# A weight conversion's mask and product merged into one VectorE operation, and three slots of a hand-written order moved

## The chip, the cores and the metric

The kernel runs on one core of a Trainium2 chip. The metric is device time in microseconds (us) of one execution, the median of three runs. The engines are named as in the profile: PE (TensorE matmul) and PEld (its weight load), DVE (VectorE), ACT (ScalarE), POOL (GpSimd), and SP, which issues DMAs.

## The reference

The computation is a chain of three blocks over 8 batches of 576 tokens, 8 heads of width 64, model width 512:

```python
q_s = softmax of q over its last axis;  k_s = softmax of k over the sequence
kv  = einsum('bhsd,bhse->bhde', k_s, v)
x   = einsum('bhsd,bhde->bhse', q_s, kv)          # linear attention, then (4608, 512)
e_idx = argmax(x @ w_gate)                        # one of 8 experts per token
out[mask] = gate_w * eom * (relu(x[mask] @ w1[e]) @ w2[e])
h   = maximum(maximum(x @ w1, x @ w2), x @ w3)    # second block, 512 -> 768
out = h @ w_out                                   # 768 -> 512
```

q, k, v and the expert weights are float32. The four weights of the last block (`m_w1`, `m_w2`, `m_w3`, `m_wo` in the kernel) are drawn as float64, so the kernel gets each number as two 32-bit words and makes a float32 of them by integer operations. That is the conversion of this document.

## The kernel before, in words

The program has two halves. In the first, up to about 580 us of the trace, attention and the first expert block run interleaved; in the second the last block runs, as a matrix product with saved multiplications (lines 1248 to 1418).

The first half is an order written out by hand in *slots*. Slot 0 to 255 each hold one matmul group of the expert block: 12 matmuls of 288 columns, either `l1_group` (x times w1, line 650, tile `hp`) or `l2_group` (h times w2, line 668, tile `yp`). 32 slots make a batch: 8 of l1, 8 of l2, 8 of l1, 8 of l2. After its group, a slot runs its *events*: the functions that `at(slot, f, ...)` put there, in the order of the calls to `at`. Each engine runs its instructions strictly in the order in which slots and events issue them.

An l1 group ends with two instructions: ACT writes the high part of `h` (line 655), and DVE the low part (line 656). The l2 groups after it need both parts of all four column blocks, so the first l2 group of eight waits, at its tenth to twelfth matmul, for the low part of the seventh l1 group, and the second l2 group for that of the eighth. An l2 group's result leaves PSUM by ACT (line 673) in the first half of a batch and by DVE (line 675) in the second. The pool of these PSUM banks has four.

Attention is cut into *units*: unit n is batch n // 2 and head half n % 2. Unit n starts at slot START[n] = 16n - 51, and STEADY says at which offset from there each of its steps runs, in the order of FRONT and BACK (lines 551 and 552). In what follows "+7" means offset 7 from the unit's start. In every unit from 4 on, the l1 groups are at +3 to +10 and l2 groups at +11 to +18 (the last three are +0 to +2 of the next unit). The steps that matter here:

- q: `q_neg` at -4 (line 233), `q_rows` on ACT, `q_inv` at +6 (lines 244 and 245), `q_norm` at +8 (line 298, DVE, tile `qn`), then at +10 and +15 `q_tr`, the transposes of `qn` on PE (line 350), and `q_lo` (line 365, DVE).
- k and v: `k_max` at -4 (line 224), `k_tr` at +0 (lines 266 to 271; the tile `dg`), `k_exp` at +1 (the PE matmul `kB` of line 278 reads `dg`), `kv_mm` and `kv_norm` at +6 (lines 325 to 337), `kv_lo` at +7 (line 343, DVE).
- `x_mm` at +13 and +17 (line 383, PE), `x_lo` at +14 and +18 (line 401, DVE).
- The expert weights: in every second slot `split_sub` (line 627, ACT) and in the slot after it `split_lo` (line 634, POOL).
- Routing, once a batch, at slots counted from the odd unit: `route_2` at +22, `route_3` at +25, `route_4` at +26 (20 small POOL instructions, lines 491 to 515), and five `route_5` at +27, 29, 31, 33, 35 (line 519, indirect DMAs that POOL issues, all into one table, each after the one before it has landed). In the terms of the next units these are +6, +9, +10 and +11, 13, 15 of an even unit and +1 and +3 of the odd unit behind it.

The conversion has 32 pieces of 128x384 numbers. Each has three steps: `dec_load` (DMA into `draw`), `dec_bits` four slots later (DVE lines 717, 719, 721 make `df` and `dp`; ACT lines 722 and 724 make `da` and `dr`; POOL lines 725 and 726 multiply and add into `dr`), and `dec_store` two slots after that (lines 734 to 736: mask, product, DMA to DRAM). DEC gives the offsets of `dec_bits` in even units (two pieces), odd units (three) and after the last unit (two). The tiles `draw`, `df`, `dp` and `da` have one buffer each, `dr` two. `dec_store` comes last among a slot's events.

Of the kernel before, what the change touches and what calls it, by code (L numbers as in the profile page):

```python
# [14 lines left out]
ALU = mybir.AluOpType  # L15
# [29 lines left out]

STEADY = ((-4, -1, -4, 0, 1, 3, 6, 6, 7, 8), (10, 10, 13, 14, 15), (15, 16, 17, 18, 19))
EARLY = {
    2: ((None, None, None, -8, -5, -3, 0, 0, 3, -1), (2, 3, 3, 7, 5), (5, 6, 7, 8, 9)),  # L50
    3: ((0, 3, 3, 5, 6, 6, 8, 8, 8, 9), (10, 10, 11, 13, 15), (13, 13, 14, 15, 16)),
# [4 lines left out]
ROUTE1 = (17, 19)  # L56

QROWS = (((-2, 4), (-1, 2), (0, 4), (2, 3), (3, 3), (4, 2), (5, 2)), 6)
DEC = ((5, 10), (3, 8, 11), (18, 26))


@with_exitstack
def tile_linear_attention__then__moe(
# [15 lines left out]
    nc = tc.nc  # L79
    dma = nc.sync.dma_start  # L80
    gdma = nc.gpsimd.dma_start
    vec = nc.vector
# [470 lines left out]
    for n, s0 in START.items():  # L553
# [3 lines left out]
        else:  # L557
            t = STEADY
        if n > 2:
# [169 lines left out]
    def dec_store():  # L729
        if not dec_m:  # L730
            return
        i, j, a2, r = dec_m.popleft()

        vec.tensor_scalar(out=a2, in0=a2, scalar1=1.125 * 2.0 ** -15, scalar2=None, op0=ALU.is_ge)
        nc.gpsimd.tensor_tensor(out=r, in0=a2, in1=r, op=ALU.mult)
        dma(out=w32_d[i][:, j], in_=r)

    dslots = [START[n] + o for n in range(4, 2 * B) for o in DEC[n % 2]] + [START[2 * B - 1] + o for o in DEC[2]]
    assert len(dslots) == 32
    for x in dslots:  # L740
        at(x - 4, dec_load)
        at(x, dec_bits)
        at(x + 2, dec_store)
# [782 lines left out]
```

## Time and profile before

| what | value |
|---|---|
| median of three runs | 1200.14 us (1200.04 to 1201.42) |
| the profiled execution's own time | 1197.52 us |
| its span, first to last instruction | 1195.5 us |
| PE busy, share of the span | 1136.8 us, 95% |
| DVE busy | 786.4 us, 66% |
| ACT busy | 583.8 us, 49% |
| POOL busy | 412.9 us, 35% |
| 32 masks on DVE (line 734), median of one | 506 ns |
| 32 products on POOL (line 735), median of one | 1030 ns |

The shares are means over the whole span. The conversion runs from 86 us to 530 us, and there DVE and POOL are far busier than their means. "Busy" of PE is the union of its matmuls, which overlap each other.

### The profile page before, as it was taken

The numbers are of one execution on the slowest core, as the hardware profiler recorded it, in microseconds if no ns is written. First come the engines' busy times: TensorE is split into PE (matmuls) and PEld (weight loads), VectorE is DVE, ScalarE is ACT, GpSimd is POOL, SyncE is SP. The second block draws the span as 40 slices with busy tenths as digits, with TensorE's granted clock in tenths as the row PEclk, the third lists the DMA queues.
The fourth block names the chain that finished last, engine by engine and source line by source line (L and its number), as shares of the span: only waits on it lengthen the run. The fifth ranks groups of instructions, "written<-read, shape, count | busy, mean of one in ns | idle before, by whom it ended". The sixth has DMA issues, their size and how long they took to land. (4 is left out here: it accounts for less than half of the span.)

```text
span 1195.5 us, 21865 instructions
## 1 busy us (share of the span) xinstructions
PE 1136.8 (95%) x7626; PEld 1061.4 (89%) x7626; DVE 786.4 (66%) x1476; ACT 583.8 (49%) x1549; POOL 412.9 (35%) x502
## 2 busy tenths in 40 slices
PE   4699999999999999999999999999999999999994
PEld 2499899898999999999998899899899989989983
DVE  7777878788787878647798566455556446554430
ACT  2466676756667676536454423443344244333220
POOL 2156857677676857787241020000000000000000
PEclk8799999999999999999999999999999999999997
DMA  6784657576565654437698478487678848747701
GB/s 160 187 226 127 195 156 212 156 221 201 160 193 165 187 143 153 135 137 249 212 320 298 160 236 287 134 295 237 225 231 266 272 147 287 237 138 235 222 19 42
DMA packets 204210, 234.97 MB, mean 197 GB/s; under 512 B 78253, under 2 KB 122061, under 8 KB 204096
## 3 DMA queue, kind: packets, MB, share of 16 engines
q1 hardware_dynamic: 202384, 233.14, 62.7%
q8 instruction: 62, 1.02, 0.4%
q0 software_dynamic: 1712, 0.39, 0.2%
q14 instruction: 52, 0.43, 0.1%
HBM read 189.56 MB, written 44.13 MB: 195 GB/s over the span
## 5 line engine op out<-in xcount | busy, mean ns | idle before, releaser
L668 PE MATMUL yp<-h,w 128*128 128x288 f32 x1536 | 222.7, 299 | 7.4 <-DVE h L656 7.4
L668 PEld LDWEIGHTS yp<-h,w 128*128 128x128 f32 x1536 | 207.7, 188 | 11.4 <-DVE h L656 8.8
L650 PE MATMUL hp<-xs,w 128*128 128x288 f32 x1536 | 217.5, 298 | 0.0
L650 PEld LDWEIGHTS hp<-xs,w 128*128 128x128 f32 x1536 | 206.9, 188 | 2.6
L634 POOL TENSOR_TENSOR w<-stg,w 128x512 fp32r<-128x512 f32 x126 | 180.3, 1436 | 79.6 <-ACT w L627 78.1
L1248 PE MATMUL pY<-t,sw 128*128 128x384 f32 (+1 forms) x972 | 193.5, 342 | 2.1 <-ACT s L1257 1.7
L1248 PEld LDWEIGHTS pY<-t,sw 128*128 128x128 f32 x972 | 172.8, 188 | 6.3 <-ACT s L1257 2.9
L1225 POOL DMA_INDIRECT out_dram<-ocx,ftb x1 | 1.0, 981 | 481.8 <-SPq L1432 481.8
L1336 PE MATMUL op<-wo,hc 128*128 128x512 f32 (+1 forms) x666 | 156.2, 394 | 0.0
L1336 PEld LDWEIGHTS op<-wo,hc 128*128 128x128 f32 (+1 forms) x666 | 125.1, 188 | 27.9
L1257 ACT ACTIVATE s<-pY 128x384 f32<-128x384 f32 (+1 forms) x108 | 53.6, 496 | 133.5 <-PE pY L1248 129.6
L656 DVE SCALAR_TENSOR_TENSOR h<-hp,h 128x288 fp32r<-128x288 f32 x128 | 57.2, 453 | 64.3 <-ACT h L655 62.3
L240 ACT ACTIVATE q<-q,qm 128x64 f32<-128x64 f32 x240 | 80.1, 337 | 0.0
L627 ACT ACTIVATE w<-stg 128x512 fp32r<-128x512 f32 x128 | 78.9, 621 | 0.0
L655 ACT ACTIVATE h<-hp 128x288 fp32r<-128x288 f32 x128 | 50.9, 398 | 40.7 <-PE hp L650 40.5
L1264 ACT ACTIVATE hc<-c 128x384 fp32r<-128x384 f32 (+1 forms) x72 | 38.2, 530 | 62.2 <-DVE c L1287 61.8
L1248 PE MATMUL pZ<-B,sw 128*128 128x384 f32 (+1 forms) x324 | 66.8, 341 | 1.5 <-DVE c L1281 1.5
L1248 PE MATMUL pY<-B,sw 128*128 128x384 f32 (+1 forms) x324 | 66.4, 340 | 0.6 <-DVE y L675 0.6
L1248 PE MATMUL pX<-B,sw 128*128 128x384 f32 (+1 forms) x324 | 66.8, 341 | 0.0
L1248 PE MATMUL pX<-t,sw 128*128 128x384 f32 (+1 forms) x324 | 66.5, 340 | 0.0
L1248 PEld LDWEIGHTS pZ<-B,sw 128*128 128x128 f32 x324 | 57.9, 188 | 3.6 <-DVE c L1281 1.8
L1257 ACT ACTIVATE sx<-pX 128x384 f32<-128x384 f32 (+1 forms) x54 | 26.9, 497 | 67.6 <-PE pX L1248 64.2
(251 smaller groups left out, 1858.7 us busy)
## 6 DMA issues: line engine op xcount, KB each, us to landing
sw<-ws_d SPq DMA_DIRECT2D x315, 256.0 KB, 3.6
stg<-in_moe_w_dram SPq DMA_DIRECT2D x31, 1024.0 KB, 5.3
ws_d<-sw SPq DMA_DIRECT2D x63, 256.0 KB, 3.2
fw<-in_moe_w_dram SPq DMA_DIRECT2D x48, 256.0 KB, 4.1
v<-in_v_dram SPq DMA_DIRECT2D x80, 128.0 KB, 4.7
draw<-in_moe_w_dram SPq DMA_DIRECT2D x24, 384.0 KB, 4.8
k<-in_k_dram SPq DMA_DIRECT2D x16, 512.0 KB, 5.5
q<-in_q_dram SPq DMA_DIRECT2D x16, 512.0 KB, 6.8
```

The costliest lines, as they stand in the source:

```text
L240: act(out=qt[:, i], in_=qt[:, i], func=ACTF.Exp, bias=u["qm"][:, i], accum_out=u["qs"][:, i])
L627: act(out=t[:, 0], in_=src, func=ACTF.Copy)
L634: eng.tensor_tensor(out=t[:, 1], in0=src, in1=t[:, 0].bitcast(F32), op=ALU.subtract)
L650: mm(ps, w[:, a, kk], xp[b, kk][:, c, cs], start=(n == 0), stop=(n == 11))
L655: act(out=h[:, 0, cs], in_=ps, func=ACTF.Relu)
L656: vec.scalar_tensor_tensor(out=h[:, 1, cs], in0=ps, scalar=0.0, in1=h[:, 0, cs].bitcast(F32), op0=ALU.max, op1=ALU.subtract,)
L668: mm(ps, w[:, a, f], ht[f][:, c, cs], start=(n == 0), stop=(n == 11))
L1225: nc.gpsimd.indirect_dma_start(out=out[:, :], out_offset=bass.IndirectOffsetOnAxis(ap=tb[0:n, 0:1], axis=0), in_=src, in_offset=None, boun ...
L1248: mm(ps[:, 0:nn], w[:, a, kap], tt_[key, kap][:, cc, 0:nn], start=(start and k == 0), stop=(k == 5), skip_group_check=True)
L1257: act(out=t[:, 0:n_of(c)], in_=pst[n, "X" if nm == "sx" else "Y"][:, 0:n_of(c)], func=ACTF.Copy)
L1264: act(out=h[:, 0, cols], in_=t[:, 0:nn], func=ACTF.Copy)
L1336: mm(ps[0:m], hc[f][:, a, col:col + m], wo[f][:, cc], start=(f == F_ORDER[0] and i == 0), stop=(f == F_ORDER[5] and i == 2))
```

## The change

The mask (line 734, a DVE comparison that overwrote `da`) and the product (line 735, POOL) become one DVE operation that reads `da` and `dr` and writes `dr`. In STEADY the last two offsets of FRONT are exchanged: `kv_lo` moves from +7 to +8 and `q_norm` from +8 to +7. In DEC the first piece of an even unit moves from +5 to +6, and the second and third of an odd unit from +8 and +11 to +10 and +13, each with its load and its store.

```diff
-STEADY = ((-4, -1, -4, 0, 1, 3, 6, 6, 7, 8), (10, 10, 13, 14, 15), (15, 16, 17, 18, 19))
+STEADY = ((-4, -1, -4, 0, 1, 3, 6, 6, 8, 7), (10, 10, 13, 14, 15), (15, 16, 17, 18, 19))
...
-DEC = ((5, 10), (3, 8, 11), (18, 26))
+DEC = ((6, 10), (3, 10, 13), (18, 26))
...
-        vec.tensor_scalar(out=a2, in0=a2, scalar1=1.125 * 2.0 ** -15, scalar2=None, op0=ALU.is_ge)
-        nc.gpsimd.tensor_tensor(out=r, in0=a2, in1=r, op=ALU.mult)
+        vec.scalar_tensor_tensor(out=r, in0=a2, scalar=1.125 * 2.0 ** -15, in1=r, op0=ALU.is_ge, op1=ALU.mult)
         dma(out=w32_d[i][:, j], in_=r)
```

On DVE in an even unit, from `q_inv` at +6 on (`qs`), before: `h` of +7, `kv_lo`, the mask, `h` of +8, `q_norm`, `h` of +9, the first of `route_3`.

```order
L245 RECIPROCAL qs<-qs 128x20
L656 SCALAR_TENSOR_TENSOR h<-hp,h 128x288
L343 TENSOR_TENSOR kvs<-kvraw_202,kvs 128x256
L734 TENSOR_SCALAR da<-da 128x384
L656 SCALAR_TENSOR_TENSOR h<-hp,h 128x288
L298 TENSOR_TENSOR qn<-q,qs 128x4x5x64
L656 SCALAR_TENSOR_TENSOR h<-hp,h 128x288
L474 TENSOR_TENSOR rz<-roh,rl 128x40
```

The same place after:

```order
L245 RECIPROCAL qs<-qs 128x20
L717 TENSOR_SCALAR df<-draw 128x384
L719 SCALAR_TENSOR_TENSOR df<-draw,df 128x384
L721 TENSOR_SCALAR dp<-df 128x384
L656 SCALAR_TENSOR_TENSOR h<-hp,h 128x288
L298 TENSOR_TENSOR qn<-q,qs 128x4x5x64
L656 SCALAR_TENSOR_TENSOR h<-hp,h 128x288
L343 TENSOR_TENSOR kvs<-kvraw_202,kvs 128x256
L734 SCALAR_TENSOR_TENSOR dr<-da,dr 128x384
L656 SCALAR_TENSOR_TENSOR h<-hp,h 128x288
L474 TENSOR_TENSOR rz<-roh,rl 128x40
```

The three conversion instructions, which stood ahead of `route_2` before, now stand between `q_inv` and the `h` of +7; `q_norm` is one `h` earlier, and `kv_lo` and the merged operation are behind it.

On DVE in an odd unit, from the `h` of +8 on, before: `q_norm`, the second piece, `h` of +9 and +10, `q_lo`, its mask.

```order
L656 SCALAR_TENSOR_TENSOR h<-hp,h 128x288
L298 TENSOR_TENSOR qn<-q,qs 128x4x5x64
L717 TENSOR_SCALAR df<-draw 128x384
L719 SCALAR_TENSOR_TENSOR df<-draw,df 128x384
L721 TENSOR_SCALAR dp<-df 128x384
L656 SCALAR_TENSOR_TENSOR h<-hp,h 128x288 x2
L365 TENSOR_TENSOR qTs<-qT,qTs 128x576
L734 TENSOR_SCALAR da<-da 128x384
L717 TENSOR_SCALAR df<-draw 128x384
```

After, from `q_norm` on, which here too stands one `h` earlier:

```order
L298 TENSOR_TENSOR qn<-q,qs 128x4x5x64
L656 SCALAR_TENSOR_TENSOR h<-hp,h 128x288
L343 TENSOR_TENSOR kvs<-kvraw_203,kvs 128x256
L656 SCALAR_TENSOR_TENSOR h<-hp,h 128x288 x2
L365 TENSOR_TENSOR qTs<-qT,qTs 128x576
L717 TENSOR_SCALAR df<-draw 128x384
L719 SCALAR_TENSOR_TENSOR df<-draw,df 128x384
L721 TENSOR_SCALAR dp<-df 128x384
L233 TENSOR_REDUCE qm<-q 128x20
L224 TENSOR_REDUCE kmx<-k 128x256
L734 SCALAR_TENSOR_TENSOR dr<-da,dr 128x384
```

The second piece has left the place between `q_norm` and the `h` of +9, and follows the `h` of +10 and `q_lo`.

On POOL in an odd unit, around its first piece, before, with the last two of the five table writes of `route_5`:

```order
L519 DMA tab_d<-tsrc,rpi 4736x4
L634 TENSOR_TENSOR w<-stg,w 128x512
L519 DMA tab_d<-tsrc,rpi 4736x4
L725 TENSOR_TENSOR dr<-dr,dp 128x384
L726 TENSOR_TENSOR dr<-dr,df 128x384
L634 TENSOR_TENSOR w<-stg,w 128x512
L735 TENSOR_TENSOR dr<-da,dr 128x384
```

After:

```order
L519 DMA tab_d<-tsrc,rpi 4736x4
L634 TENSOR_TENSOR w<-stg,w 128x512
L519 DMA tab_d<-tsrc,rpi 4736x4
L725 TENSOR_TENSOR dr<-dr,dp 128x384
L726 TENSOR_TENSOR dr<-dr,df 128x384
L634 TENSOR_TENSOR w<-stg,w 128x512 x4
```

The product of line 735 is gone from POOL; the multiply and the add of the piece stand where they stood, behind the last table write.

## Rows read from the trace of the kernel before

**Rows 1.** Stretches: length; busy time (and instructions) per engine; granted clock; DMA share, GB/s.

```profile
100.00:490.00 390.00, 379.82 (x3217) 358.90 (x3217) 320.60 (x571) 254.61 (x840) 284.41 (x333) 1.00 0.61 179
490.00:580.00 90.00, 90.00 (x692) 89.26 (x691) 55.33 (x107) 43.80 (x105) 64.73 (x73) 1.00 0.49 168
```

**Rows 2.** Waits of PE from 75 to 580: total us, times, longest.

```profile
PE yp L668 <- DVE h L656: 7.4, 6, 1.6
PE qT L350 <- DVE qn L298: 1.8, 2, 1.0
```

**Rows 3.** Timeline of PE in odd unit 9: start, us, instruction, [idle before].

```profile
279.50 0.66 PE L350 MATMUL qT<-ident,qn 128*128 128x128 f32 x4
...
280.29 1.60 PE L668 MATMUL yp<-h,w 128*128 128x288 f32 x10
283.18 3.71 PE L668 MATMUL yp<-h,w 128*128 128x288 f32 x26 [1.28 <-DVE h L656]
```

**Rows 4.** Timeline of DVE in odd unit 9.

```profile
271.30 0.44 DVE L734 TENSOR_SCALAR da<-da 128x384 f32<-128x384 f32 x1
...
277.17 2.28 DVE L298 TENSOR_TENSOR qn<-q,qs 128x1280 f32<-128x1280 f32 x1
279.37 1.43 DVE L717 TENSOR_SCALAR df<-draw 128x384 int32<-128x384 int32 x1
...
282.68 0.82 DVE L656 SCALAR_TENSOR_TENSOR h<-hp,h 128x288 fp32r<-128x288 f32 x2
```

**Rows 5.** Timeline of POOL in odd unit 9.

```profile
272.54 0.99 POOL L519 DMA_INDIRECT tab_d<-tsrc,rpi  x1 [1.02 <-DMA tab_d<-tsrc,rpi]
273.55 1.03 POOL L725 TENSOR_TENSOR dr<-dr,dp 128x384 f32<-128x384 f32 x1
274.66 1.02 POOL L726 TENSOR_TENSOR dr<-dr,df 128x384 f32<-128x384 f32 x1
275.64 1.48 POOL L634 TENSOR_TENSOR w<-stg,w 128x512 fp32r<-128x512 f32 x1
```

**Rows 6.** By tile: count, duration ns min/median/max, first and last start.

```profile
L719 DVE SCALAR_TENSOR_TENSOR df<-draw,df x32: 557/559/1534, 99.5 to 519.9; 128x384 int32<-128x384 int32 x32
L734 DVE TENSOR_SCALAR da<-da x32: 348/506/1740, 106.5 to 521.5; 128x384 f32<-128x384 f32 x32
L634 POOL TENSOR_TENSOR w<-stg,w x126: 1272/1302/2537, 54.7 to 570.8; 128x512 fp32r<-128x512 f32 x126
L298 DVE TENSOR_TENSOR qn<-q,qs x16: 1491/2208/2282, 23.4 to 482.6; 128x1280 f32<-128x1280 f32 x16
```

**Rows 7.** Short stretches of DVE alone: length, busy (instructions), clock, DMA share, GB/s.

```profile
237.70:239.15 1.45, 1.32 (x4) 1.00 0.00 0
272.90:275.00 2.10, 1.81 (x6) 1.00 0.80 310
292.20:293.05 0.85, 0.81 (x2) 1.00 1.57 140
```

**Rows 8.** Timeline of DVE in even unit 8.

```profile
244.35 2.23 DVE L298 TENSOR_TENSOR qn<-q,qs 128x1280 f32<-128x1280 f32 x1
246.51 0.44 DVE L656 SCALAR_TENSOR_TENSOR h<-hp,h 128x288 fp32r<-128x288 f32 x1
...
249.09 0.46 DVE L656 SCALAR_TENSOR_TENSOR h<-hp,h 128x288 fp32r<-128x288 f32 x1 [0.29 <-ACT h L655]
```

**Rows 9.** Timeline of PE in even unit 8.

```profile
247.43 4.78 PE L668 MATMUL yp<-h,w 128*128 128x288 f32 x34
```

**Rows 10.** Timeline of DVE and POOL at +12 of even unit 8.

```profile
256.23 0.51 DVE L734 TENSOR_SCALAR da<-da 128x384 f32<-128x384 f32 x1
...
256.60 1.00 POOL L726 TENSOR_TENSOR dr<-dr,df 128x384 f32<-128x384 f32 x1
```

**Rows 11.** Timeline of DVE, and of PE, before the matmul `kB` of unit 10.

```profile
294.62 1.86 DVE L271 TENSOR_SCALAR dg<-ident,m 128x128 f32<-128x128 f32 x2
...
296.62 0.67 PE L278 MATMUL kB<-dg,ones 128*128 128x256 f32 x2
```

## The prediction

> **What bounds the kernel now.** I read the stretches first. The change acts from 100 to 490 us, where PE is busy for 379.82 of 390 us, DVE for 320.60 and POOL for 284.41, at full granted clock; right behind it, almost without attention steps, PE is busy for all of 90 us [rows 1]. So PE sets the pace, about 10 us of the stretch are idle, and DVE is close behind at 82%. The change leaves PE's instructions and their order as they are in this stretch, so it can only alter how long PE waits.
>
> The table of waits tells which waits end last. 7.4 us (6 times) are an l2 group waiting for the low part of `h` from DVE, and 1.8 us (twice) a transpose waiting for `qn` from DVE [rows 2], together 9.2 of the 10 us. One of the six in detail, odd unit 9: PE starts the first l2 group (+11) at 280.29, runs ten matmuls and starts the next at 283.18 [rows 3]. DVE shows why: `q_norm` started at 277.17 and took 2.28, the second piece of the conversion followed from 279.37 on, and only then, at 282.68, came the `h` of +9 and +10 [rows 4]. Even units have no such gap: in unit 8 the 34 matmuls recorded from 247.43 on run in one go [rows 9].
>
> **The change part by part.**
>
> *The slots in odd units.* The second piece leaves the place ahead of the `h` of +9, and `q_norm` is one slot earlier. By itself this removes the wait in each of six odd units, at most the 7.4 us of [rows 2].
>
> *The merged operation's own duration.* The trace has no such operation, but line 719 is one of the same form on the same engine and of the same shape: 557 ns at least, 1534 at most, against 348 to 1740 for the mask [rows 6]. By the shortest ones a piece costs 0.21 us more, 32 pieces 6.7 us of DVE; by the medians, 559 against 506, 1.7 us. I take 0.2 us a piece, by the shortest. Where DVE has idle time ahead of it, none of it is on PE's path.
>
> *The product off POOL.* That is 32 instructions that no longer run there. PE waits for nothing that POOL writes in this stretch [rows 2], so I cost the gain itself at nothing. It might relieve DVE: the three bit instructions of a piece took 3.3 us of DVE behind `q_norm` in unit 9 and 1.3 us in the gap of unit 8 [rows 4, 7], and `q_norm` 1491 to 2282 ns [rows 6]; the long ones lie beside POOL work.
>
> [...]
>
> *The wait that the merged operation adds.* The mask needed only `da`, from ACT. The merged operation also reads `dr`, which POOL's add (line 726) writes. DVE, in order, now waits for POOL, and behind it in DVE's queue are `h`, `kv_norm`, `q_inv` and `q_norm`, on which PE depends. Three places:
>
> 1. Odd units, +5. DVE ran the mask of unit 9's first piece at 271.30 [rows 4]; POOL finished that piece's add at 274.66 + 1.02 = 275.68, since the five table writes of `route_5`, each waiting for the landing of the one before, stood ahead of it [rows 5]. In this order DVE waits 4.4 us. POOL's next weight operation follows the add without a gap (275.64) and may hold the merged one up for its 1.3 us more. From 275.7 on: merged operation 0.56 (or 1.3 later), `h` 0.4, `kv_norm` and `q_inv` 2.0 [rows 7], `h` 0.4, `q_norm` 1.5 to 2.3 [rows 6]: `qn` is there at 280.6 to 282.7. PE began the transposes at 279.50 [rows 3]; so it waits 1.1 to 3.2 us there, less up to 0.5 if PE itself comes later than now. That replaces the 283.18 - 281.75 = 1.4 us by which the eleventh matmul was late (ten matmuls at 0.14 us from 280.29). Net, -0.8 to +1.8.
> 2. Even units, +12. The mask started at 256.23, POOL's add ended at 257.60 [rows 10]. DVE waits about 1.4 us, with the y additions and `x_lo` behind it; the four PSUM banks cover those. What counts is `dg` at the next unit's +1.
> 3. Odd units, +15. The third piece's bits are now issued at +13, behind `k_max` and the second merged operation; the multiply and add behind them need 2.1 us of POOL [rows 5], beside which DVE has only `x_lo` to run, 0.8 us [rows 7]. A wait of 1.3 us stands ahead of `q_lo`, `k_tr` and `dg`. `dg` has no slack: it ends at 296.48, and `kB` starts at 296.62 [rows 11]. The earlier `q_norm` takes part of this back.
>
> For 1 and 3 together I take +0.5 us an odd unit, the middle of 1's ends, since DVE's lead from there can pay for 3.
>
> *The slots in even units.* The first piece's bits stood at +5, where DVE has gaps. Now they stand in the dense row behind `q_inv`: 1.3 us [rows 7]. POOL's multiply and add, 1.0 us each [rows 5], then meet `q_norm` and `kv_lo`, and a weight operation of 1.3 us meets the merged one. In unit 8 the `h` of +9 is written from 246.51 to 246.95 [rows 8]. PE needs it ten matmuls into the group that starts at 247.43 [rows 9]; at 4.78 us for 34, ten are 1.4 us, so at 248.8: a slack of 1.9 us. Against it stand 1.3 for the bits, 0.2 for the merged form, 1.0 for the multiply, 0.5 for what is left of the add, 1.3 for the weight operation; less 1.1, since the row ahead of `q_inv` starts earlier without the bits, and less the 0.7 that `q_norm` lost beside POOL before (2.23 against 1.49). That is 2.5 us, a stall of 0.6. The `h` of +10, before at 249.09, comes behind `route_3`'s chain and costs PE about 0.7 more. Less 0.2 us of transposes that no longer wait: +1.1 an even unit; between -0.2 (DVE goes ahead of POOL each time) and +2.
>
> *Sum.* Six even units at +1.1 and six odd at +0.5 are +9.6 us. Unit 4's wait for `qn`, the 1.0 of [rows 2], goes with the earlier `q_norm`, and the last odd unit has no next `dg`, -0.6. In all +8 us on the profiled execution's 1197.5 us (its span of 1195.5 and 2.0 around it): 1205.5. The median of the runs lies 2.6 us above the profiled one, so 1208.
>
> **Rivals.**
>
> *The waits go and nothing comes (faster).* If POOL's add is done by the time DVE gets there, the 9.2 us of [rows 2] go: 1191. For it: the slots are moved away from the very place where DVE was late, and POOL loses 32 instructions. Against it: at +5 of odd units POOL's add ended 4.4 us behind the mask, and neither that slot nor the POOL order ahead of it changes.
>
> *An exchange.* Even units keep their slack, and in odd units a wait for `qn` of about the same length takes the place of the wait for `h`: within 2.4 us of 1200.
>
> *DVE becomes the bound (slower by more).* If POOL's weight operation goes ahead of the merged one each time and the late `dg` is not absorbed, a pair of units costs 1.1 + 1.9 = 3.0 us, six pairs 18: 1218. It decides once DVE reaches `dg` more than about 1 us later than now.
>
> **How the numbers follow.** Forecast 0.52, faster rival 0.24, exchange 0.14, large loss 0.10. The ends of the bounds, six times (-0.2 - 0.8) less 1.6 and six times (2 + 1.8) less 1.6, are -7.6 and +21. A range of 1190 to 1217 leaves out the lower edge of the first rival and the upper part of the last; as cases of both signs hold much of the chance, the forecast's own range is 1203 to 1213. What a measurement can tell from no change is 0.2%, 2.4 us. Faster than that: 0.25; within: 0.13; slower: 0.62.
>
> **What would show it.** In the profile after: DVE idle ahead of the merged operation of 3 to 5 us at +5 of odd units and about 1 us at +12 of even units, released by POOL's `dr`; PE waits for `qn` at line 350 in odd units in place of those for `h` at line 668; waits for `h` at line 668 in even units that were not there; `kB` later, behind `dg`. If the merged operation hardly waits, or DVE's idle time ahead of `q_norm` takes its wait up, the forecast is wrong and the time goes to 1191. If no even unit waits for `h`, the +1.1 is wrong.

## The result and the profile after

| kernel | median, us | runs |
|---|---|---|
| before | 1200.14 (1199.07 to 1203.23) | 5 |
| after | 1216.8 (1216.15 to 1224.74) | 5 |

The ratio is 1.0149, 95% interval 1.0117 to 1.0181: slower by some 17 us. The forecast was 1208. The profiled execution of after is the longest of its five, 1224.74 us (span 1223.0); the other four lie between 1216.15 and 1216.92.

The stretches first, as in [rows 1], and behind them two short ones (length, busy time per engine, granted clock, DMA share, GB/s):

```profile
100.00:490.00 390.00, 368.43 (x3051) 347.69 (x3050) 289.60 (x547) 244.65 (x800) 243.88 (x293) 0.98 0.60 173
490.00:580.00 90.00, 88.53 (x704) 86.19 (x703) 49.96 (x97) 46.05 (x119) 65.14 (x73) 1.00 0.47 150
...
292.60:296.00 3.40, 3.40 (x17) 3.40 (x16) 3.33 (x7) 2.03 (x5) 1.76 (x2) 0.51 1.15 323
309.70:313.10 3.40, 3.40 (x15) 3.22 (x14) 1.80 (x3) 1.33 (x2) 0.02 (x1) 0.50 0.45 150
```

PE is idle for 22 us of the 390 instead of 10, and runs 166 instructions fewer in them. The last two rows are new: PE is busy for all of 3.4 us, at half clock. There are six such stretches in this execution, from 162.9, 234.6, 292.6, 309.7, 586.2 and 640.8 on; before shows none between 75 and 700.

The waits of PE from 75 to 600 (total us, times, longest), against [rows 2]:

```profile
PE xT L383 <- DVE qTs L365: 17.8, 11, 2.2
PE qT L350 <- DVE qn L298: 4.7, 4, 1.5
PE hp L650 <- DVE h L656: 2.8, 1, 2.8
PE yp L668 <- ACT y L673: 0.5, 1, 0.5
```

The waits of l2 groups for `h` from DVE are gone. In their place stands one that no step of the prediction has: `x_mm` waits for `qTs`, the result of `q_lo`, 17.8 us in all. PE's waits rose from 9.2 to 25.8 us, 16.6 more. Six stretches of 3.4 us at half clock cost at most 1.7 us each against full clock, 10.2. The sum is 26.8, and the span grew by 27.5. The last two of the six stretches and the wait for `h` (at 585) lie behind the conversion; the other four executions are 8 us shorter, and their mean granted clock (0.983 to 0.987 against 0.982) fits fewer such stretches, but their traces were not taken. Why these two came I did not test.

What DVE waited for, same stretch:

```profile
DVE dr L734 <- POOL dr L726: 37.4, 19, 4.0
DVE df L717 <- DMA draw<-in_moe_w_dram: 10.3, 4, 3.5
```

The first row is the wait that the prediction put at the centre. The second is not in it: the bits of a piece wait for its load. Three places show what each does.

*Odd units, +5.* Timeline of POOL, DVE and PE in odd unit 9 of after:

```profile
284.57 1.01 POOL L726 TENSOR_TENSOR dr<-dr,df 128x384 f32<-128x384 f32 x1
285.54 2.86 POOL L634 TENSOR_TENSOR w<-stg,w 128x512 fp32r<-128x512 f32 x2
...
285.61 1.63 DVE L734 SCALAR_TENSOR_TENSOR dr<-da,dr 128x384 f32<-128x384 f32 x1 [4.03 <-POOL dr L726]
...
289.66 1.48 DVE L298 TENSOR_TENSOR qn<-q,qs 128x1280 f32<-128x1280 f32 x1
...
291.20 0.66 PE L350 MATMUL qT<-ident,qn 128*128 128x128 f32 x4 [1.49 <-DVE qn L298]
```

DVE stands for 4.03 us, the merged operation takes 1.63 beside POOL's next one, and PE waits 1.49 for `qn`. This is as forecast: 4.4, up to 1.3 on top of 0.56, and 1.1 to 3.2. In the other five odd units DVE stands for 2.1 to 3.9 us, and PE waits 1.4, 0.9 and 1.0 us in three of them and not at all in two.

*From +12 of an even unit to +1 of the odd one.* Timeline of POOL, DVE and PE at the change from unit 8 to 9:

```profile
267.82 1.30 POOL L634 TENSOR_TENSOR w<-stg,w 128x512 fp32r<-128x512 f32 x1
...
266.29 0.56 DVE L734 SCALAR_TENSOR_TENSOR dr<-da,dr 128x384 f32<-128x384 f32 x1 [0.66 <-POOL dr L726]
266.76 0.81 DVE L675 TENSOR_TENSOR y<-yp,y 128x288 f32<-128x288 f32 x2
267.49 2.25 DVE L401 TENSOR_TENSOR xs<-xr,xs 128x576 fp32r<-128x576 f32 x1
...
270.39 0.74 DVE L365 TENSOR_TENSOR qTs<-qT,qTs 128x576 fp32r<-128x576 f32 x1
...
271.19 1.05 PE L383 MATMUL xT<-qTs,kvs 128*128 128x288 f32 x6 [1.30 <-DVE qTs L365]
272.13 0.67 PE L278 MATMUL kB<-dg,ones 128*128 128x256 f32 x2
272.45 1.95 PE L668 MATMUL yp<-h,w 128*128 128x288 f32 x12
```

The wait for the add is short, but `x_lo` now falls beside POOL's operations and takes 2.25 us, and `q_lo` behind it comes 1.3 us too late for `x_mm`. At the same place before, `x_lo` took:

```profile
257.40 0.82 DVE L401 TENSOR_TENSOR xs<-xr,xs 128x576 fp32r<-128x576 f32 x1
```

*The third piece, from +9 of an odd unit to +1 of the even one.* Timeline of SP (its issues), DVE and PE, unit 9 to 10:

```profile
289.40 0.44 SPq L194 DMA_DIRECT2D k<-in_k_dram  x1
...
292.23 4.92 SPq L210 DMA_DIRECT2D v<-in_v_dram  x4
297.24 1.35 SPq L214 DMA_DIRECT2D v<-in_v_dram  x1
298.70 0.45 SPq L704 DMA_DIRECT2D draw<-in_moe_w_dram  x1
...
302.96 0.36 DVE L717 TENSOR_SCALAR df<-draw 128x384 int32<-128x384 int32 x1 [3.48 <-DMA draw<-in_moe_w_dram]
...
306.98 1.61 DVE L734 SCALAR_TENSOR_TENSOR dr<-da,dr 128x384 f32<-128x384 f32 x1 [2.00 <-POOL dr L726]
308.51 0.74 DVE L365 TENSOR_TENSOR qTs<-qT,qTs 128x576 fp32r<-128x576 f32 x1
...
309.31 1.50 PE L383 MATMUL xT<-qTs,kvs 128*128 128x288 f32 x6 [1.94 <-DVE qTs L365]
310.61 1.05 PE L278 MATMUL kB<-dg,ones 128*128 128x256 f32 x2
311.10 2.87 PE L668 MATMUL yp<-h,w 128*128 128x288 f32 x12
```

The load of the third piece moved with its bits, from +7 to +9, and there it is issued behind the nine loads of `k`, `q` and `v` of a coming unit, which take SP from 289.40 to 298.6. In before it was issued ahead of them:

```profile
282.44 0.33 SPq L704 DMA_DIRECT2D draw<-in_moe_w_dram  x1
282.83 0.43 SPq L194 DMA_DIRECT2D k<-in_k_dram  x1
```

In after its data come at about 302.9; DVE is idle for 3.48 us, then waits 2.00 for the add, takes 1.61, and only then runs `q_lo`. PE waits 1.94. Then the clock: `x_mm`, `kB` and the l2 group take 1.50, 1.05 and 2.87 here, and 1.05, 0.67 and 1.95 at the same place of the fence above, 1.75 us more for the same work.

The merged operation by tile (count, duration ns min/median/max), against the mask in [rows 6]:

```profile
L734 DVE SCALAR_TENSOR_TENSOR dr<-da,dr x32: 543/1610/1640, 108.6 to 544.2; 128x384 f32<-128x384 f32 x32
```

543 at least, as line 719's 557 had said; the 1610 are those, 19 of the 32, where POOL's weight operation follows the add at once, as at 285.54.

### The profile page after: what moved, and what is told of

The parts are those of the page before. It is cut to its first block, busy times and chain, and to the rows that moved or that the text cites. A ratio compares the mean times of both kernels' runs of the same rounds, so it can differ in the third digit from the quotient of the medians.

```text
span 1223.0 us, 21812 instructions
## 1 busy us (share of the span) xinstructions
PE 1149.6 (94%) x7626; PEld 1072.1 (88%) x7626; DVE 770.2 (63%) x1476; ACT 586.0 (48%) x1549; POOL 382.7 (31%) x470
## 5 line engine op out<-in xcount | busy, mean ns | idle before, releaser
L668 PE MATMUL yp<-h,w 128*128 128x288 f32 x1536 | 227.2, 303 | 0.5 <-ACT y L673 0.5
L668 PEld LDWEIGHTS yp<-h,w 128*128 128x128 f32 x1536 | 212.0, 191 | 4.8 <-DVE h L656 1.2
L634 POOL TENSOR_TENSOR w<-stg,w 128x512 fp32r<-128x512 f32 x126 | 177.2, 1416 | 101.5 <-ACT w L627 97.0
L734 DVE SCALAR_TENSOR_TENSOR dr<-da,dr 128x384 f32<-128x384 f32 x32 | 38.1, 1190 | 39.7 <-POOL dr L726 37.4
```

What stands on the lines that cost most here:

```text
L634: eng.tensor_tensor(out=t[:, 1], in0=src, in1=t[:, 0].bitcast(F32), op=ALU.subtract)
L668: mm(ps, w[:, a, f], ht[f][:, c, cs], start=(n == 0), stop=(n == 11))
L734: vec.scalar_tensor_tensor(out=r, in0=a2, scalar=1.125 * 2.0 ** -15, in1=r, op0=ALU.is_ge, op1=ALU.mult)
```

## The experiments

My theory after the result: the third piece's load on SP's queue made most of the loss, the merged operation's wait for POOL's add a smaller part. The rival: the wait alone, as predicted, and the load harmless. Times are compared with runs of the kernel before on the same chip; its medians were 1199.2, 1198.05, 1197.1 and 1197.98 us for the four groups (e1 to e4, e5 to e8, e9 to e11, e12), so the ratio is what counts.

| kernel | median, us | ratio to before, 95% |
|---|---|---|
| e1 merged, old slots | 1205.95 | 1.0051 [1.0031, 1.0071] |
| e2 new slots, two operations | 1225.94 | 1.0210 [1.0188, 1.0233] |
| e3 third piece at +18 | 1204.05 | 1.0041 [1.0025, 1.0058] |
| e4 exchange in STEADY alone | 1199.09 | 0.9998 [0.9986, 1.0010] |
| e5 third load ahead of the unit's | 1201.91 | 1.0038 [1.0022, 1.0053] |
| e6 two operations, other slots | 1195.91 | 0.9983 [0.9972, 0.9993] |
| e7 merged, the slots of e6 | 1199.91 | 1.0018 [1.0007, 1.0030] |
| e8 e2 with e5's order of loads | 1214.71 | 1.0159 [1.0128, 1.0190] |
| e9 e5, two merged operations later | 1194.62 | 0.9978 [0.9963, 0.9993] |
| e10 e5, the same two left as mask and product | 1213.88 | 1.0144 [1.0124, 1.0164] |
| e11 e7, one merged operation later | 1195.49 | 0.9990 [0.9981, 0.9999] |
| e12 e9, the third one later too | 1193.37 | 0.9956 [0.9943, 0.9970] |

**The parts of the change, each alone.** e1 is after with the old tables:

```diff
-STEADY = ((-4, -1, -4, 0, 1, 3, 6, 6, 8, 7), (10, 10, 13, 14, 15), (15, 16, 17, 18, 19))
+STEADY = ((-4, -1, -4, 0, 1, 3, 6, 6, 7, 8), (10, 10, 13, 14, 15), (15, 16, 17, 18, 19))
-DEC = ((6, 10), (3, 10, 13), (18, 26))
+DEC = ((5, 10), (3, 8, 11), (18, 26))
```

> Only the mask and product are merged; all slots are those of before. Wait theory (the merged operation's wait for POOL's add is the cause): DVE idles 4 to 5 us ahead of it at +5 of each odd unit, about 1.4 us at +12 of even units, and the time is 1205 to 1212. Slot theory (the moved slots, above all the third piece of odd units, whose load now stands on SP's queue behind the nine loads of a unit): hardly slower than before, 1200 to 1203. Duration theory (the merged operation's 1.6 us beside POOL work): 1203 to 1207 with waits that PE does not see.

e2 is before with the new tables:

```diff
+STEADY = ((-4, -1, -4, 0, 1, 3, 6, 6, 8, 7), (10, 10, 13, 14, 15), (15, 16, 17, 18, 19))
+DEC = ((6, 10), (3, 10, 13), (18, 26))
```

> Mask on DVE and product on POOL as before; the slots of after. Wait theory: no wait of DVE for POOL's add, so PE's waits of before go and few come, 1190 to 1197. Slot theory: the third piece's load still lands late, DVE idles about 2 us an odd unit ahead of line 717 and x_mm at +1 of even units waits about 1.5 us, 1200 to 1207. Duration theory: 1191 to 1198.

e4 is before with that line of STEADY and the old DEC.

> Only q_norm and kv_lo change places; mask, product and conversion slots as before. All theories: a small gain, since q_norm runs one slot sooner and the bits behind it end about 1 us sooner, so the waits of 7.4 and 1.8 us shrink: 1193 to 1199. If the wait for h at line 668 does not shrink, 1200.

e4: nothing, 0.9998; `h` is still waited for, 8.8 us. So the exchange neither helps nor harms by itself. e1: the merged operation alone costs 0.5%, as the wait theory had it, and PE's waits of e1 show how; half clock came with them in four stretches of 3.4 us (from 100 to 490 us the mean granted clock was 0.98):

```profile
PE qT L350 <- DVE qn L298: 16.0, 12, 3.1
```

e2: the slots alone cost more than the whole change, 2.1%, and more than any of the theories gave. The waits of PE in e2, and SP and DVE at the third piece of unit 9:

```profile
PE xT L383 <- DVE qTs L365: 22.0, 5, 6.7
PE kB L278 <- DVE dg L271: 5.7, 11, 1.0
```

```profile
296.38 6.11 SPq L210 DMA_DIRECT2D v<-in_v_dram  x4
302.58 0.46 SPq L214 DMA_DIRECT2D v<-in_v_dram  x1
303.14 0.44 SPq L704 DMA_DIRECT2D draw<-in_moe_w_dram  x1
...
307.40 0.36 DVE L717 TENSOR_SCALAR df<-draw 128x384 int32<-128x384 int32 x1 [4.64 <-DMA draw<-in_moe_w_dram]
```

There is no merged operation in e2, and `x_mm` waits even longer: a late load is enough for that. The rival, that the load is harmless, has fallen. It also follows that merging is worth something in the new slots (2.1% against 1.5%), though it costs in the old ones.

**The third piece.** e3 puts it at +18, so that its load stands behind the unit's nine but has time; e5 leaves it and lets the unit's loads start a slot later:

```diff
-    dslots = [START[n] + o for n in range(4, 2 * B) for o in DEC[n % 2]] + [START[2 * B - 1] + o for o in DEC[2]]
+    dslots = [START[n] + (18 if o == 13 and n < 2 * B - 1 else o) for n in range(4, 2 * B) for o in DEC[n % 2]]
+    dslots += [START[2 * B - 1] + o for o in DEC[2]]
```

> After, but the third piece of odd units (except the last) is at +18 instead of +13, its load at +14, its store at +20, where DVE has gaps. Slot theory: the draw wait and the wait ahead of q_lo go, x_mm at +1 of even units no longer waits (9 to 12 us of the 17.8 us of that wait), 1203 to 1209. Wait theory: the waits at +5 of odd and +12 of even units stay, as does x_mm at +1 of odd units (about 1.6 us each); the third piece is one of three places, 1209 to 1213.

```diff
-            at(LOAD.get(n, START.get(n - 2, 0) + 9), load_unit, b, hb)
+            at(LOAD.get(n, START.get(n - 2, 0) + (10 if n % 2 else 9)), load_unit, b, hb)
```

> After, but the nine loads of a unit are issued at +10 of an odd unit instead of +9, so that the third piece's draw load (+9) stands ahead of them on SP's queue; nothing else moves. Queue theory (the third piece is late because its load stands behind the unit's loads): DVE's idle time ahead of line 717 for draw, 12.6 us in the profile of after, falls under 4 us, x_mm's wait at +1 of even units (2.2 to 2.9 us each) mostly goes, 1203 to 1209. POOL theory (the third piece's wait for POOL's add ahead of q_lo is what makes x_mm late): the draw wait goes, but x_mm still waits 1.5 us or more at +1 of even units, 1212 to 1217.

Both take away 1.1 points of the 1.5. e5 is the clean one: no instruction of PE, DVE, ACT or POOL moves against after, only SP's order. SP in e5 at unit 9:

```profile
287.15 0.33 SPq L704 DMA_DIRECT2D draw<-in_moe_w_dram  x1
287.53 1.56 SPq L194 DMA_DIRECT2D k<-in_k_dram  x1
```

and the waits of PE in e5:

```profile
PE xT L383 <- DVE qTs L365: 7.9, 6, 1.3
PE qT L350 <- DVE qn L298: 6.0, 5, 1.6
```

DVE no longer waits for that load, no stretch has half clock (the mean granted clock of the execution is 0.989, in after 0.982), and `x_mm` at +1 of the even units no longer waits; the six waits for `qTs` that are left are those at +1 of odd units. So the order of one load on SP's queue is worth 1.1%, 13 us, the half clock included; 1201.9 lies 1.1 us below the queue theory's range.

e8 gives e2 the same order of loads.

> The slots of after with mask and product apart, and the third piece's draw load ahead of the unit's loads on SP's queue. Queue theory: the 44 us of DVE idle time ahead of line 717 in the run with the slots alone fall to a few us, and the 26 us that it lost are nearly all back: 1194 to 1203. If the slots themselves crowd DVE ahead of q_lo: 1210 or more.

It gains 0.5% over e2 and still stands at 1.6%, so the queue theory's range is missed: with two operations the new slots lose elsewhere too (PE waits for `dg` 12.1 us, 11 times, for `qTs` 5.4). DVE's waits for `draw` fell from 44.1 us to 18.2, not to a few, because a second load is late, that of the second piece. POOL, SP and DVE of e8 in unit 9:

```profile
287.12 1.19 POOL L735 TENSOR_TENSOR dr<-da,dr 128x384 f32<-128x384 f32 x1
...
288.34 0.32 SPq L736 DMA_DIRECT2D w_d<-dr  x1
...
289.23 0.40 SPq L704 DMA_DIRECT2D draw<-in_moe_w_dram  x1
...
292.46 0.36 DVE L717 TENSOR_SCALAR df<-draw 128x384 int32<-128x384 int32 x1 [2.15 <-DMA draw<-in_moe_w_dram]
```

The store of the first piece waits on SP's queue until POOL's product ends, at 288.31, and the load of the second piece stands behind it. In the old slots that load was at +4, ahead of the store at +5; in the new ones it is at +6. In after and e5 DVE does not wait for it. In each pair with the same slots and loads DVE waits more for `draw` with two operations than merged: 4.3 us in before and 0.7 in e1, 44.1 in e2 and 12.6 in after, 18.2 in e8 and 0.8 in e5, 24.0 in e6 and 0.9 in e7. How much of e8's 1.6% this makes was not tested.

**The wait for POOL's add.** e6 has the two operations and e7 the merged one, both with the exchange and with DEC's pieces at +5, +10 and +3, +11, +18 (the last odd unit's third at +13):

```diff
+DEC = ((5, 10), (3, 11, 18), (18, 26))
```

> Mask on DVE and product on POOL as before, q_norm and kv_lo exchanged, and DEC = ((5, 10), (3, 11, 18)): the second piece of odd units is out of the way of h, and the third stands in the next even unit's first slots. Both theories: the waits of PE for h and qn of before (9.2 us) go and no draw wait comes, 1189 to 1195. If a conversion instruction of DVE between +11 and +17 is what makes x_mm or kB late, 1197 to 1202.

> As the run with split operations and DEC = ((5, 10), (3, 11, 18)), but mask and product merged on DVE. Wait theory: DVE idles about 4 us at +5 of odd units and about 1 us at +12 of even units, x_mm or q_tr wait in odd units, so 6 to 12 us above that run: 1197 to 1205. If the merged operation's wait is harmless once no load is late, within 3 us of that run.

e6 is 0.17% faster than before, 0.9 us short of its range: the waits for `h` and `qn` are gone, but DVE waits 24.0 us for `draw` and PE 4.4 for `dg`. The merged operation costs 0.35% there, 4 us, between the two sizes expected of e7: e7 waits for `qn` 5.1 us, 5 times, e6 never. e11 is e7 with the merged operation of the odd units' first piece at +7, when the add has ended:

```diff
-        at(x + 2, dec_store)
+        at(x + (4 if x + 51 < 32 * B and (x + 51) % 32 == 19 else 2), dec_store)
```

> Merged operations with the conversion pieces of e7 (even +5 and +10, odd +3, +11, +18; 1199.9 us), the merged operation of the odd units' first piece at +7 instead of +5. If that one wait for POOL's add is the 4 us by which e7 is behind the same places with split operations (1195.9), its waits for qn (5.1 us, 5 times) go and the time is 1193 to 1197. If the merged operation costs by its duration or by other places, it stays at 1198 to 1202.

The waits for `qn` are gone and with them 0.28%, nearly all that e7 was behind. e9 does the same to e5, for the odd units' first piece (+5 to +7) and the even units' second (+12 to +14):

```diff
-        at(x + 2, dec_store)
+        at(x + (4 if x + 51 < 32 * B and (x + 51) % 32 in (10, 19) else 2), dec_store)
```

> The changed kernel with the odd units' load_unit at +10 (so the third piece's load stands ahead of it, as in e5_draw_ahead_of_unit, 1201.9 us), and with two of the merged operations two slots later: that of the odd units' first piece at +7 instead of +5, that of the even units' second piece at +14 instead of +12. POOL's add is done by then. If what is left of the loss over e5's split-operation level is DVE's wait for POOL's add, the waits for qn (6.0 us, 5 times) and for qTs (7.9 us, 6 times) go, DVE's waits for POOL fall from 38.5 to under 20 us, and the time is 1188 to 1195. If the wait only follows to the next thing (the store's late place holds up h of +8, kv_lo or dg), the time stays at 1199 to 1204.

The waits of PE in e9:

```profile
PE xT L383 <- DVE qTs L365: 4.7, 6, 1.2
PE yp L668 <- DVE h L656: 1.4, 2, 0.9
```

DVE's waits for the add fell from 38.5 to 19.5 us, those of PE for `qn` went, the six for `qTs` that are left stand at +1 of even units, behind the third piece, and the kernel is faster than before by 0.2%. The two later operations made 0.6%, 7 us. e12 puts the third one behind the add as well (+15 to +19):

```diff
+        o = (x + 51) % 32
+        at(x + (2 if x + 51 >= 32 * B else 4 if o in (10, 19) else 6 if o == 29 and x + 51 < 32 * B - 3 else 2), dec_store)
```

> e9_late_stores (1194.6 us), and in the odd units up to 13 the merged operation of the third piece at +19 instead of +15. In e9 that operation is the last one ahead of q_lo at +15 that still waits (1.99 us for POOL's add, then 1.63), and xT waits for qTs 4.7 us, 6 times, at +1 of the next even unit. If the wait for POOL's add is the cause there too, that wait goes and the time is 1189 to 1193. If the store's later place costs as much (the piece after it shares its one buffer), it stays at 1193 to 1197.

The waits for `qTs` fell to 1.1 us, `kB` waits 2.2 for `dg` instead; 1193.37 lies at the border of the two expectations. At 0.9956 it is the fastest kernel here, 0.44% below before; against e9 the intervals touch, so this last step's own gain is not settled.

**Where it costs to leave the product on POOL.** e10 tries the other cure for e5's two waits, mask and product apart:

```diff
+        if split:
+            vec.tensor_scalar(out=a2, in0=a2, scalar1=1.125 * 2.0 ** -15, scalar2=None, op0=ALU.is_ge)
+            nc.gpsimd.tensor_tensor(out=r, in0=a2, in1=r, op=ALU.mult)
+        else:
...
+        at(x + 2, dec_store, x + 51 < 32 * B and (x + 51) % 32 in (10, 19))
```

> As e9's starting point (the changed kernel with the odd units' load_unit at +10), stores at their places, but the odd units' first piece and the even units' second piece keep the mask on DVE and the product on POOL; the others stay merged. The mask doesn't wait for POOL's add. If the wait for the add is what the merged operation costs, the waits for qn and qTs at odd +1 go and the time is 1190 to 1196. If the product on POOL, with its store behind it on SP, costs as much as the wait (as the split operations did in e8), the time is 1200 to 1208.

Both expectations missed: 1.4% slower than before, far above e5. DVE, POOL and PE of e10 at the change from unit 8 to 9:

```profile
259.16 3.29 DVE L401 TENSOR_TENSOR xs<-xr,xs 128x576 fp32r<-128x576 f32 x1
...
259.56 1.31 POOL L634 TENSOR_TENSOR w<-stg,w 128x512 fp32r<-128x512 f32 x1
260.81 1.03 POOL L736 TENSOR_TENSOR dr<-da,dr 128x384 f32<-128x384 f32 x1
...
263.91 1.05 PE L383 MATMUL xT<-qTs,kvs 128*128 128x288 f32 x6 [1.97 <-DVE qTs L365]
```

`x_lo` ends after both POOL operations, and takes 3.29 us; without the product it took 2.25 in after, and 0.76 in e9, where it is through before POOL's weight operation starts. The 3.29 us are roughly a sum: 0.76 and the two POOL operations of 1.31 and 1.03 are 3.10. PE waits 1.97, and half clock (0.5) follows in four of the units. By the table of waits PE waits little longer in all than in e5 (17.1 us against 15.9); the half clock, 17.1 us of it and so at most 8.5 us of time, is enough for the 6.8 us by which the span is longer. The store behind the product on SP is not the reason: DVE waits only 0.8 us for `draw`. What the product costs here is the DVE operation that stands beside it, and the half clock behind that.

Not tried: a second buffer for `draw` or `da`.

## Why the prediction was wrong

The direction was right; the size was not: +16.7 us measured, +8 forecast, and most of the forecast was put where nothing happened, so that the direction came out is in part luck.

- *The slots in odd units*: right. The waits of [rows 2] for `h` are gone in after, and unit 4's wait for `qn` too. What else the change did hid the gain until e9, which waits 1.4 us there.
- *The wait at +5 of odd units*: right in mechanism, in size at its lower end or under it: 4.03 us on DVE and 1.5 on PE in unit 9, but 2.1 to 4.0 and 0 to 1.5 over the six units; e11 shows its price in e7's slots, 0.28%.
- *The wait at +12 of even units, "the four PSUM banks cover those"*: wrong. They cover the y additions; `x_lo` and `q_lo` stand in the same row, and `x_mm` at +1 of the odd unit waits for them, 1.3 us each time, 7.9 in e5. The wait for the add itself was 0.7 us, not 1.4. I looked at `dg` as the next thing that counts, and the matmul ahead of `kB` came first.
- *The third piece*: this is the step that failed. I wrote that a wait of 1.3 us for POOL "stands ahead of `q_lo`, `k_tr` and `dg`", and paid for it out of the earlier `q_norm`. The bits' own wait for their load was not in it: the load had moved from +7 to +9, past the unit's nine loads, and I gave that no term. It is the largest of all, 1.1% or 13 us (e5 against after): DVE waits 1.5 to 3.5 us for the load in five odd units, then 2.0, not 1.3, for POOL's add, and `x_mm` waits 1.5 to 2.2 us at +1 of the five even units behind them, with half clock after some of these waits.
- *The even units' `h`, +1.1 each, 6.6 in all*: wrong. No l2 group waits for `h` in after. That POOL's operations add their whole length to DVE's here (the terms of 1.0, 0.5 and 1.3) was an estimate, and no run shows these terms: in unit 8 of after `q_norm` took 2.09 us against 1.48 in unit 9, `kv_lo` 0.87 against 0.41 in unit 8 of before, and the merged operation 1.63 against 0.56 at 266.29, together 2.1 us more in place of 2.8. Which other terms behind the +1.1 were too large I did not separate; the row's delay did not outlast the slack of 1.9 us of [rows 8, 9].
- *The product off POOL, "at nothing"*: right in the old slots, where e1 has only the loss; wrong in the new ones, where after is 0.6 points better than e2, and e5 is 1.2 better than e8. The prediction looked at what PE and DVE get from POOL, and not at the store and the loads behind the product on SP's queue.
- *The clock* had no term: I priced stalls by their length alone. In the profiled execution half clock came to at most 10 us on top of 16.6 of stalls.

The rival "the waits go and nothing comes" is what e9 and e12 make of the change, once the load and the late operations are put in order: 0.2% and 0.44% below before, against 0.76% (1191) worked out for it. "DVE becomes the bound" gave nearly the time measured, 1218, with the late `dg` as its place; the place was `q_lo`, just ahead of it, and the first reason a load, so that the numbers lie close is luck.

## What to carry to other kernels

When a step moves in a hand-written order, list its DMAs with it, and read on the issuing queue what they are moved past: here a load that slipped behind nine others was late by their whole issue time, 9 us, and one that slipped behind a store waited for what the store waited for (the end of POOL's product at 288.31 in e8, with 2.15 us of idle DVE behind it). When two operations on two engines are merged into one that reads both, issue the merged one where the slower input is already there: moving one by two slots gave back 0.28 of the 0.35% that it cost in e7, and moving two of them gave 0.6% in e5. Look also at what a moved operation comes to stand beside: taking work off POOL gained nothing in the old slots, and gained in the new ones, where the product held up a DVE operation on PE's path (3.29 us for `x_lo` in e10, 2.25 in after) or a load on SP's queue (e8).

## What the runs showed of the hardware

After some stalls of PE its granted clock fell to 0.5 for 3.4 us in the middle of a busy stretch: six times in after, four in e1 and in e10 (one of 6.8 us), three in e8 (one of 6.8; the mean granted clock of the execution was 0.979), five times 6.8 us in e2, once 6.8 in e4, and never in before, e3, e5, e6, e7, e9, e11 and e12 (between 75 and 700 us). Idle times just ahead of it were 1.49 us (292.6) and 1.94 (309.7) in after, and 1.97 in e10; but the wait of 2.21 us that ended at 450.99 in after was not followed by it, nor were two of the six of 1.95 to 1.99 in e10, so the length of one stall does not tell. When a stall is followed by a fall is left open.

The other surprise is that the merged operation of after takes one of two times. It took 1.60 to 1.64 us in 19 cases, all with POOL's weight operation right behind the add, whether DVE had waited (13) or not (6). It took 0.54 to 0.56 us in the other 13, where POOL was idle as it started or went on to a table write of line 519, as at 266.29. That is three times the price for the same 128x384 numbers, and in all 32 cases what POOL did next tells which of the two it was.
